# Convolution, SoLU layer and LayerNorm in one kernel: w_in scaled while it is decoded, two chunks convolved in float32, row sums from the product

## The chip, the cores and the metric

The kernel runs on one core of a Trainium2 chip. The metric is the device time of one execution in microseconds. Lower is better. The two weight matrices w_in and w_out are float64 arrays, the other inputs float32. The kernel reads the former as pairs of 32-bit words and decodes exponent, mantissa and sign itself.

## The reference

```python
# x: 8 x 4160 x 192 float32; weight: 8 heads x 7 taps
w = softmax of weight over its 7 taps
out[b, s, h, :] = sum over k of w[h, k] * x_pad[b, s + k, h, :]   # causal, 24 channels a head
x = out.reshape(33280, 192)
h = x @ w_in                                   # 192 x 1024
sm = exp(h - max h) / (sum of exp + 1e-9)
solu = h * sm
ln = (solu - mean) / sqrt(var + 1e-6) * g_ln   # over the 1024 columns
return (ln @ w_out).astype(float32)            # 1024 x 192
```

## The kernel before

The 33280 rows are 260 tiles of 128 rows. They come in 17 chunks: the first batch as 1024, 1056 and 2080 rows, each later batch as two of 2080. For a chunk, x is loaded in windows of 112 rows (plus 16 rows of overlap), five windows to a piece `xr` (`load`, line 125). `sum_squares` gives a scale `s` for the chunk: squares on ScalarE in chunks 0 and 1, maxima on VectorE from chunk 2 on. `halve_steps` splits each piece, times `s`, into a high and a low float16 half (`xs`, lines 211 to 227, nearly all on POOL). `product` (line 260) multiplies them with band matrices `taps_hi` and `taps_lo`, three float16 matmuls for each head, into PSUM. `upper` (ScalarE, line 280) and `lower` (VectorE, line 289) write the result as float16 halves `y`, and `turn` (line 312) transposes them by DMA into `yT`.

A tile then goes through these steps:

- `emit_h` (line 714): ten matmuls of 512 columns on the float16 halves `whi` and `wlo` of w_in give the 1024 logits `ph` in PSUM;
- `emit_max` (line 725, VectorE) scales `ph` and takes its extremum, with an accumulator; `emit_exp` (line 732, ScalarE) writes `e` and its sum;
- `emit_mul` (line 785, VectorE) writes h e over `e`; `emit_hi` (line 790, ScalarE) and `emit_lo` (line 799, POOL) split it into float16 halves `p`, which a DMA transposes into `pT` (line 801);
- `emit_square` (line 794, ScalarE) sums the squares;
- five tiles later `emit_out` (line 813): 24 matmuls with the halves `ohi` and `olo` of the centred w_out. These have 194 columns: 192 of w_out, one of ones, which gives the row's sum, and one of zeros. `emit_evac` (line 821) copies the result out of the one PSUM bank `po`;
- every eight tiles `Group.roots` (lines 867 to 877, POOL) and `row` (lines 882 and 886) scale the rows and store them.

The order is that of the program: `step(i)` issues the work around tile i in a fixed order to the engines' in-order queues, with the tile before it (`cur`) in the steps from the product on. SyncE issues all DMAs, also in order. `chores` spreads the next chunks' work over a chunk's tiles by the fractions in its tables; `chain` and `Queue` hold the scale's steps and the POOL halving.

Before tile 0 the program decodes w_in (`Words`: exponents, mantissas, low words, signs; POOL adds mantissa and low word), sums its squares, takes a power of two `t_in` as its scale and splits it. w_out is decoded beside the first tiles: `out_values` multiplies by the gains, then `out_squares`, `out_mean` (line 674, ones-matmuls in float32) and `out_halves` (lines 689 to 696) centre, scale and split it. In steps 0 to 2 a tile's product stands in its own step (`WARM = 3`), and step 3 has none.

## Time and profile before

| | before |
|---|---|
| median of 3 runs | 1287.07 us (1286.88 to 1289.79) |
| profiled execution, and its span | 1289.18 us, 1287.5 us |
| busy: TensorE, VectorE, ScalarE, POOL | 93%, 78%, 73%, 77% |
| granted TensorE clock, mean | 0.982 |
| DMA queue 1: packets, bytes, share of 16 engines | 724318, 221 MB, 88.3% |

A line of the groups or of the timeline names the source line, engine, operation, out<-in tiles and shapes. In the timeline the first two numbers are the start and the duration in us, and the bracket at the end is how long the engine was idle before, and what ended that. PE is TensorE's matmuls, PEld its weight loads, DVE VectorE, ACT ScalarE, SPq SyncE's queue. A float32 matmul is recorded as two.

### The profile page before, as it was taken

How to read it: one execution, taken by the hardware profiler on the slowest of the kernel's cores; microseconds unless marked ns; L12 is line 12 of the kernel's file. 1: busy time of each engine (PE TensorE's matmuls, PEld its weight loads, DVE VectorE, ACT ScalarE, POOL GpSimd, SP SyncE). 2: the span in 40 equal slices, each digit the busy share in tenths (PEclk: the TensorE clock that was granted, in tenths of full speed). 3: DMA queues.
4: the chain of work that ended last, by engine and by line, in shares of the span. 5: the costliest groups of instructions: out<-in, count | busy, mean ns of one | idle time of the engine just before them, and what ended most of it. 6: DMA issues, size and time to landing. Idle time of an engine off the chain costs nothing. (4 is left out here: it accounts for less than half of the span.)

```text
span 1287.5 us, 25290 instructions
## 1 busy us (share of the span) xinstructions
PE 1195.9 (93%) x9334; PEld 848.4 (66%) x9334; DVE 999.2 (78%) x1881; ACT 937.3 (73%) x1507; POOL 984.9 (77%) x935
## 2 busy tenths in 40 slices
PE   2567899799999999999999999999999999999996
PEld 1344576577777677777776677667676767767675
DVE  8965798578787888878787878788787777776666
ACT  6465677577877777787877777787777778777773
POOL 6543769597897869798896969798796979866665
PEclk9888999899999999999999999999999999999998
DMA  7365798889989898999979899998979898897977
GB/s 212 66 145 117 142 195 159 169 168 187 204 162 210 160 211 176 186 202 171 212 146 203 163 196 198 169 195 158 214 146 201 190 175 157 153 171 144 189 157 145
DMA packets 724442, 222.78 MB, mean 173 GB/s; under 512 B 650894, under 2 KB 724062, under 8 KB 724190
## 3 DMA queue, kind: packets, MB, share of 16 engines
q1 hardware_dynamic: 724318, 221.17, 88.3%
q8 instruction: 73, 1.20, 0.4%
q14 instruction: 51, 0.42, 0.1%
HBM read 33.00 MB, written 25.56 MB: 45 GB/s over the span
## 5 line engine op out<-in xcount | busy, mean ns | idle before, releaser
L799 POOL TENSOR_TENSOR p<-e,p 128x1024 f16<-128x1024 f32 x258 | 551.0, 2138 | 243.9 <-ACT p L790 243.1
L813 PE MATMUL po<-ohi,pT 128*128 128x194 f16 x4160 | 571.3, 248 | 17.7 <-DVE raw L821 7.6
L813 PEld LDWEIGHTS <-pT 128*128 128x128 f16 x6240 | 534.8, 98 | 73.2 <-DMA pT<-p 14.3
L813 PE MATMUL po<-olo,pT 128*128 128x194 f16 x2080 | 512.6, 246 | 0.8 <-DVE olo L696 0.8
L725 DVE TENSOR_SCALAR_CACHE_REDUCE ph<-ph,cv 128x1024 f32<-128x1024 f32 x248 | 320.0, 1291 | 177.3 <-PE ph L714 176.6
L714 PEld LDWEIGHTS <-yT 128*128 128x128 f16 x2600 | 251.4, 98 | 278.5 <-DMA yT<-y 20.7
L732 ACT ACTIVATE e<-ph,sm 128x1024 f32<-128x1024 f32 x259 | 288.0, 1112 | 176.2 <-DVE ph L725 166.0
L714 PE MATMUL ph<-whi,yT 128*128 128x512 f16 x1560 | 385.5, 383 | 19.5 <-DMA yT<-y 16.8
L790 ACT CAST p<-e 128x1024 f16<-128x1024 f32 x259 | 269.3, 1040 | 115.1 <-DVE e L785 68.6
L785 DVE SCALAR_TENSOR_TENSOR e<-ph,cv,e 128x1024 f32<-128x1024 f32 x247 | 315.5, 1277 | 1.4 <-ACT e L732 1.3
L714 PE MATMUL ph<-wlo,yT 128*128 128x512 f16 x1040 | 269.8, 382 | 4.5 <-DVE wlo L612 4.5
L794 ACT ACTIVATE sq<-e 128x1024 f32<-128x1024 f32 x259 | 273.0, 1054 | 0.0
L289 DVE SCALAR_TENSOR_TENSOR y<-pc,y 112x456 f16<-112x456 f32 (+4 forms) x156 | 80.4, 533 | 63.4 <-ACT y L280 55.0
L227 POOL TENSOR_TENSOR xs<-xr,xs 128x960 f16<-128x960 f32 (+1 forms) x63 | 121.8, 1934 | 2.5
L821 DVE COPY raw<-po 128x194 f32<-128x194 f32 x257 | 89.8, 350 | 3.0 <-PE po L813 3.0
L280 ACT ACTIVATE y<-pc 112x456 f16<-112x456 f32 (+2 forms) x140 | 68.2, 499 | 32.5 <-PE pc L260 11.1
L260 PE MATMUL pc<-xs,taps_hi 128*112 128x456 f16 (+1 forms) x256 | 69.5, 353 | 14.3 <-POOL xs L227 6.1
L166 DVE TENSOR_REDUCE xa<-xr 128x1 f32<-128x384 f32 x120 | 73.0, 619 | 0.0
L224 POOL TENSOR_SCALAR xr<-xr,s 128x960 f32<-128x960 f32 (+1 forms) x63 | 65.8, 1045 | 1.9
L886 DVE TENSOR_SCALAR_CACHE_REDUCE o<-raw,t 128x192 f32<-128x192 f32 x133 | 53.1, 404 | 12.7 <-POOL t L877 12.7
L260 PEld LDWEIGHTS <-taps_hi 128*112 128x112 f16 x288 | 37.0, 139 | 38.4 <-issue 8.9
L213 POOL TENSOR_SCALAR xs<-xr,s 128x960 f16<-128x960 f32 (+1 forms) x54 | 55.7, 1032 | 4.4 <-DVE s L101 4.4
(152 smaller groups left out, 633.8 us busy)
## 6 DMA issues: line engine op xcount, KB each, us to landing
out_dram<-o SPq DMA_DIRECT2D x128, 192.0 KB, 2.7
xr<-in_x_dram SPq DMA_DIRECT2D x41, 480.0 KB, 4.6
xr<-in_x_dram SPq DMA_DIRECT2D x22, 384.0 KB, 3.9
pT<-p SPq DMA_TRANSPOSE x259, 4.5
yT<-y SPq DMA_TRANSPOSE x99, 3.8
raw_out<-in_moe_w_out_dram SPq DMA_DIRECT2D x1, 1536.0 KB
raw_in<-in_moe_w_in_dram SPq DMA_DIRECT2D x1, 1024.0 KB, 9.0
xr<-in_x_dram SPq DMA_DIRECT2D x8, 84.0 KB, 3.5
```

Of the source, the lines that this page charges most:

```text
L227: (2.1 * size + 0.2, lambda: pool.tensor_tensor(xl, r, h, ALU.subtract)),
L260: nc.tensor.matmul(o, taps[:, h + j, :], r, start=q == 0, stop=q == len(ops) - 1)
L289: dve.scalar_tensor_tensor(self.at(D, h * HD, e, z, a, b), pc[:, :, e:z], 1.0 / TAPS, self.at(0, h * HD, e, z, a, b), ALU.mult, ALU.subtract,)
L714: nc.tensor.matmul(t.ph[:, n * 512 : (n + 1) * 512], lhs, w[:, r, n * 512 : (n + 1) * 512], start=(j == 0), stop=(j == len(ops) - 1),)
L725: dve.tensor_scalar(t.ph, t.ph, t.cv[:, 0:1], None, ALU.mult, ALU.min, accum_out=t.bias)
L732: act.activation(t.e, t.ph, AF.Exp, bias=t.bias, scale=-1.0, accum_out=grp.z[:, g : g + 1])
L785: dve.scalar_tensor_tensor(t.e, t.ph, t.cv[:, 3:4], t.e, ALU.mult, ALU.mult)
L790: act.copy(t.p16[:, :, 0, :], t.halves)
L794: act.activation(junk, t.e, AF.Square, accum_out=t.grp.s2[:, t.g : t.g + 1])
L799: eng.tensor_tensor(t.p16[:, :, 1, :], t.halves, t.p16[:, :, 0, :], ALU.subtract)
L813: nc.tensor.matmul(t.po[:, 0:WX], t.pT[:, a, :], w[:, c, :], start=(j == 0), stop=(j == len(ops) - 1),)
L821: dve.tensor_copy(t.grp.raw[:, t.g, :], t.po[:, 0:WX])
```

## The change

- w_in: its top rows come in two transfers. `largest` takes the maximum of the raw high words' magnitudes while the words arrive; the power of two `t_in` is worked out from that and added to the exponents' bias (`bias_in`), so the decoded values are already scaled. `join` (VectorE) puts mantissa and low word together in place of POOL's two steps. Two of `whi`'s blocks are copied between partitions by DMA.
- Chunks 0 and 1 (`exact`) are convolved from the unscaled float32 pieces with float32 `taps`: one matmul in place of three, with the chunk's scale applied in `upper` and `lower`. Chunk 2 takes its scale from squares on ScalarE, no longer from maxima on VectorE.
- w_out: its scale comes from the squares of the decoded exponents and the largest gain; the work is spread over steps 0 to 2 in another order. The products of tiles 0 to 2 stand one step later, as all others do, and tile 0's low half is VectorE's.
- The row sum comes from an accumulator in `emit_mul`; `ohi` and `olo` have 192 columns.
- The pool of `xr` has 9 buffers, not 11; `emit_h` takes the blocks in another order; the reciprocal in `root_power` goes.

On POOL (GpSimd), from its last memset on: before, w_in's decoding, chunk 0's and chunk 1's halving stand among the first tiles' low halves `p`.

```order
L485 TENSOR_SCALAR m_in<-m_in 128x1024
L490 TENSOR_TENSOR f_in<-m_in,raw_in 128x1024
L485 TENSOR_SCALAR m_in<-m_in 128x512
L490 TENSOR_TENSOR f_in<-m_in,raw_in 128x512
L224 TENSOR_SCALAR xr_1_87<-xr_1_87,s_164 128x960
L227 TENSOR_TENSOR xs_180<-xr_1_87,xs_180 128x960
L609 TENSOR_SCALAR whi<-f_in,t_in 64x512 x2
L485 TENSOR_SCALAR m_out<-m_out 128x1536
L490 TENSOR_TENSOR f_out<-m_out,raw_out 128x1536
L213 TENSOR_SCALAR xs_329<-xr_0_94,s_298 128x960
L224 TENSOR_SCALAR xr_0_94<-xr_0_94,s_298 128x960
L799 TENSOR_TENSOR p_0_333<-e_330,p_0_333 128x2x512
```

On POOL, the same place in the changed kernel; the last rows are chunk 2's first piece.

```order
L514 TENSOR_TENSOR f_out<-m_out,raw_out 128x1536
L810 TENSOR_TENSOR p_1_399<-e_344,p_1_399 128x2x512
L810 TENSOR_TENSOR p_2_465<-e_407,p_2_465 128x2x512
L810 TENSOR_TENSOR p_3_547<-e_462,p_3_547 128x2x512
L810 TENSOR_TENSOR p_4_614<-e_544,p_4_614 128x2x512
L810 TENSOR_TENSOR p_5_673<-e_611,p_5_673 128x2x512
L217 TENSOR_SCALAR xr_0_282<-xr_0_282,s_592 128x960
L220 TENSOR_TENSOR xs_681<-xr_0_282,xs_681 128x960
```

One operation of w_out is left of the decoding, the halving of chunk 1 is gone, and tile 0's low half has left the engine.

On VectorE, before, from tile 0's product to tile 1's: w_out's values stand ahead of tile 1's maximum.

```order
L785 SCALAR_TENSOR_TENSOR e_330<-ph_304,cv_165,e_330 128x1024
L505 SCALAR_TENSOR_TENSOR e_out<-raw_out,e_out 128x1536
L642 SCALAR_TENSOR_TENSOR f_out<-f_out,gl,e_out 128x192 x8
L725 TENSOR_SCALAR ph_382,sm_393<-ph_382,cv_165 128x1024
L289 SCALAR_TENSOR_TENSOR y_0_203<-pr_349,y_0_203 112x5x64
L289 SCALAR_TENSOR_TENSOR y_0_203<-pr_349,y_0_203 112x5x32
L289 SCALAR_TENSOR_TENSOR y_0_203<-pr_362,y_0_203 112x5x32
L289 SCALAR_TENSOR_TENSOR y_0_203<-pr_362,y_0_203 112x5x64
L785 SCALAR_TENSOR_TENSOR e_402<-ph_382,cv_165,e_402 128x1024
```

On VectorE in the changed kernel, from tile 1's maximum to tile 1's product.

```order
L733 TENSOR_SCALAR ph_331,sm_342<-ph_331,cv_194 128x1024
L793 SCALAR_TENSOR_TENSOR e_326,s_0_300<-ph_304,cv_194,e_326 128x1024
L529 SCALAR_TENSOR_TENSOR e_out<-raw_out,e_out 128x1536
L681 SCALAR_TENSOR_TENSOR f_out<-f_out,gl,e_out 128x192 x8
L810 TENSOR_TENSOR p_0_347<-e_326,p_0_347 128x2x512
L665 TENSOR_REDUCE osq<-gl 128x1
L666 TENSOR_TENSOR osq<-osq 128x1
L667 TENSOR_TENSOR osq<-osq 128x1
```

Tile 1's maximum now stands ahead of tile 0's product and of w_out's values, tile 0's low half behind them; the product has a second output, its row sum.

On ScalarE, before, from tile 2's exp to tile 3's.

```order
L732 ACTIVATE e_434,z_300<-ph_421,sm_432 128x1024
L790 CAST p_2_437<-e_434 128x2x512
L794 ACTIVATE sq_442,s_0_301<-e_434 128x1024
L693 ACTIVATE ohi<-f_out,t_out 128x4x192 x2
L280 ACTIVATE y_1_485<-pc_0_0_486 112x10x48
L732 ACTIVATE e_497,z_300<-ph_474,sm_493 128x1024
```

On ScalarE in the changed kernel, between the same two exps.

```order
L740 ACTIVATE e_407,z_299<-ph_387,sm_405 128x1024
L805 ACTIVATE sq_414,s_0_301<-e_344 128x1024
L172 ACTIVATE xj_1_416,xa_382<-xr_0_94 128x576
L172 ACTIVATE xj_3_418,xa_382<-xr_1_96 128x576
L172 ACTIVATE xj_0_424,xa_423<-xr_0_282 128x384
L172 ACTIVATE xj_1_426,xa_423<-xr_0_282 128x576
L172 ACTIVATE xj_2_428,xa_423<-xr_1_284 128x384
L285 ACTIVATE y_1_441<-pc_0_0_442,s_421 112x5x96
L740 ACTIVATE e_462,z_299<-ph_430,sm_448 128x1024
```

Two sums of chunk 1 and three of chunk 2 (`xj`) stand between the exps now, and the output's high halves have moved ahead of tile 2's exp.

The diff, cut to its core:

```diff
...
 
         bits = dst.bitcast(I32)
-        half = 127 << 22
         return [
             lambda: dve.tensor_scalar(dst, src, tiny, 1.0 / num, ALU.max, ALU.mult),
-            lambda: dve.reciprocal(dst, dst),
             lambda: dve.tensor_scalar(
                 bits, bits, EXPO, 1, ALU.bitwise_and, ALU.logical_shift_right
             ),
-            lambda: dve.tensor_scalar(bits, bits, float(half), None, ALU.add),
+            lambda: dve.tensor_scalar(
+                bits, bits, -1.0, float(380 << 22), ALU.mult, ALU.add
+            ),
             lambda: dve.tensor_scalar(bits, bits, EXPO, None, ALU.bitwise_and),
         ]
...
             q = nc.sync
             a, z = self.cuts[j], self.cuts[j + 1]
             t = xp.tile(
-                [P, PW, D], F32, name=f"xr_{self.ch}_{j}", tag="xr", bufs=11
+                [P, PW, D], F32, name=f"xr_{self.ch}_{j}", tag="xr", bufs=9
             )
             self.raw[j] = t
             first = (self.b * S + self.t0 - HALO) * D
...
             for j in range(n):
                 o = pc[:, :, j * HD : (j + 1) * HD]
                 sl = slice((h + j) * HD, (h + j + 1) * HD)
+                if self.exact:
+                    piece = self.raw[self.cuts.index(a)][:, 0 : z - a, sl]
+                    ops.append((0, j, o, taps, piece))
+                    continue
                 xh, xl = (q[:, a:z, sl] for q in (self.xh, self.xl))
                 ops += [
                     (0, j, o, taps_hi, xh), (2, j, o, taps_hi, xl), (1, j, o, taps_lo, xh)
                 ]
             if bank_given:
                 ops.sort(key=lambda q: q[:2])
-            for q, (_, j, o, taps, r) in enumerate(ops):
+            for q, (_, j, o, tp, r) in enumerate(ops):
                 nc.tensor.matmul(
-                    o, taps[:, h + j, :], r, start=q == 0, stop=q == len(ops) - 1
+                    o, tp[:, h + j, :], r, start=q == 0, stop=q == len(ops) - 1
                 )
             return pc
+        def scale(self):
+            return self.s[0:CW] if self.exact else 1.0 / TAPS
...
     nc.sync.dma_start(wb, weight.partition_broadcast(TJ))
     for j in range(chunks[0].np):
         chunks[0].load(j)
-    nc.sync.dma_start(
-        raw_in[:, 0:F, :].rearrange("p f t -> p (f t)"), w_in[0 : 2 * R, :]
-    )
+    for j in range(NH):
+        nc.sync.dma_start(
+            raw_in[:, j * 512 : (j + 1) * 512, :].rearrange("p f t -> p (f t)"),
+            w_in[0 : 2 * R, j * F : (j + 1) * F],
+        )
...
+    taps = cp.tile([P, H, CW], F32, name="taps")
...
+    def words(c):
+        wi.mantissas(c)
+        wi.exponents(c)
+        wi.join(c)
+    def valued(c):
+        wi.signs(c)
+        wi.value(c, dve)
...
+    for j, c in enumerate(halves):
+        wi.largest(c, floor[:, j : j + 1])
+        words(c)
+        if j == 0:
+            for f in chain0[1:-4]:
+                f()
+    wi.largest(Z, floor[:, 2:3])
+    dve.tensor_reduce(iq[:, 0:1], floor, AX.X, ALU.max)
+    dve.tensor_scalar(
+        iq[:, 0:1].bitcast(I32), iq[:, 0:1].bitcast(I32), 0x7FF00000, None,
+        ALU.bitwise_and,
+    )
+    dve.tensor_scalar(
+        iq[:, 0:1].bitcast(I32), iq[:, 0:1].bitcast(I32), 8.0,
+        -896.0 * 2.0**23, ALU.mult, ALU.add,
+    )
+    dve.tensor_tensor(iq[:, 1:2], iq[:, 0:1], iq[:, 0:1], ALU.mult)
+    tp = total(iq[:, 1:2], "wi")
...
+    dve.tensor_scalar(
+        bias_in, t_in.bitcast(I32), 1.0, -(916.0 + 127.0) * 2.0**23,
+        ALU.mult, ALU.add,
+    )
+    for c in halves:
+        wi.powers(c, bias_in)
+    c0.open(0, None)
+    settle(*spans0[0], got0)
...
+    words(Z)
+    wi.powers(Z, bias_in)
+    for c in halves:
+        valued(c)
+    for pc, hg in got0:
+        c0.upper(pc, *hg)
+    valued(Z)
...
+    for c in halves:
+        act.copy(whi[:, 0, c], wf[:, c])
+        lower_in(wlo[:, 0, c], wf[:, c], whi[:, 0, c])
+    nc.sync.dma_start(whi[top, 2, :], whi[low, 0, :])
+    nc.sync.dma_start(whi[low, 1, :], whi[top, 0, :])
+    act.copy(whi[top, 1, 0:HF], wf[top, Z])
...
+    def out_squares():
+        junk = sp.tile([P, F], F32, name="oj", tag="sq", bufs=1).bitcast(F16)
+        act.activation(
+            junk[:, 0 : NFC * D], wo.e.bitcast(F32), AF.Square, scale=2.0**20,
+            accum_out=osq[:, 0:1],
+        )
+    def out_scale():
+        gm = osq[:, 1:2]
+        dve.tensor_reduce(gm, gl, AX.X, ALU.max, apply_absolute_value=True)
+        dve.tensor_tensor(gm, gm, gm, ALU.mult)
+        dve.tensor_tensor(gm, gm, osq[:, 0:1], ALU.mult)
+        tp = total(gm, "wo", mean)
...
         ops = [
-            (y[0], whi, 0), (y[1], whi, 1), (y[2], whi, 2), (y[0], wlo, 0),
+            (y[0], whi, 0), (y[0], wlo, 0), (y[2], whi, 2), (y[1], whi, 1),
             (y[1], wlo, 1),
         ]
...
     def emit_mul(t):
-        dve.scalar_tensor_tensor(t.e, t.ph, t.cv[:, 3:4], t.e, ALU.mult, ALU.mult)
+        dve.scalar_tensor_tensor(
+            t.e, t.ph, t.cv[:, 3:4], t.e, ALU.mult, ALU.mult,
+            accum_out=t.grp.s1[:, t.g : t.g + 1],
+        )
...
-            s1 = self.raw[:, :n, D]
+            s1 = self.s1[:, :n]
...
         c1, c2, c3 = (chunks[ch + j] if ch + j < NCH else None for j in (1, 2, 3))
         if c1:
-            stage(c1, *((0.4, 0.65, 0.8), (0.19, 0.6, 0.8), (0.25, 0.75, 0.95),
+            stage(c1, *((0.375, 0.7, 0.85), (0.19, 0.6, 0.8), (0.25, 0.75, 0.95),
                         (0.0625, 0.65, 0.9))[min(ch, 3)])
         if c2 and ch < 3:
-            sums(c2, *((0.125, 0.35), (0.0, 0.4), (0.0, 0.25))[ch])
+            sums(c2, *((0.3, 0.55), (0.0, 0.4), (0.0, 0.25))[ch])
         if c3:
             put(0.5 if ch == 0 else 0.0, 0.9 if ch < 2 else 0.7, "load",
                 [(c3, j) for j in range(c3.np)])
...
-    WARM = 3
-    outs = {3: 0, 4: 1, 6: 2, 8: 3}
+    outs = {3: 0, 4: 1, 5: 2, 7: 3}
+    c1_sums = [
+        lambda h=h: chunks[1].sum_squares(*h)
+        for j in range(chunks[1].np) for h in chunks[1].halves(j)
+    ] if NCH > 1 else []
     def step(i):
         t = tiles[i] if i < NT else None
-        cur = i if i < WARM else i - 1 if i > WARM else NT
-        cur = tiles[cur] if cur < NT else None
+        cur = tiles[i - 1] if 0 < i <= NT else None
         k = outs.get(i, None) if i < DEPTH + 4 else i - DEPTH
         done = tiles[k] if k is not None and k < NT else None
         work = {}
...
         if convs:
             first = convs[0][0], conv(*convs[0])
         add_up(i, first[0].bank if first else None)
-        if i == NT - 1:
+        if i in (2, NT - 1):
             emit_mul(cur)
             emit_hi(cur)
+        if i == 2:
+            out_upper()
         if t:
             emit_max(t)
         if i == 0:
+            wo.exponents(W)
+            settle_rest()
+            wo.whole(W)
+        if i < 4:
             run_chain(20)
-        if i == 1:
-            settle_rest()
         if first:
             first[0].upper(first[1][0], *first[1][1])
             first[0].lower(first[1][0], *first[1][1])
         if t:
             (emit_exp if i < NT - 1 else last_exp)(t)
-        if cur and i < NT - 1:
+        if cur and i != 2 and i < NT - 1:
             emit_mul(cur)
             emit_hi(cur)
         if i == 0:
-            queue.run(2.0)
+            wo.powers(W, rebias)
+            out_squares()
+        if i == 1:
             out_values()
         if cur and cur.grp.n == 1 and i < NT:
             emit_z(cur)
...
             if i == NT - 1:
                 emit_evac(done)
         if cur and i < NT:
-            emit_lo(cur, pool if i < NT - 1 else dve)
+            emit_lo(cur, pool if 1 < i < NT - 1 else dve)
         if i == NT - 1:
             emit_z(t)
             last_split(t)
         run_chain(6 if t and t.n < 12 else 4)
-        if i == 0:
-            upper_rest()
+        if i == 1:
+            out_scale()
+        if i == 2:
+            out_lower()
         if done and done.grp.n > 1 and i != NT - 1:
             emit_evac(done)
         run_rows(i)
...
             second[0].lower(second[1][0], *second[1][1])
         if cur and i < NT:
             emit_square(cur)
-        if i == 1:
-            out_squares()
-        if i == 2:
-            out_mean()
-            out_halves()
+        if i in (1, 2):
+            for f in c1_sums[i - 1 :: 2]:
+                f()
+            if i == 2 and c1_sums:
+                follow(chunks[1], i)
         for c, h in work.get("sum", []):
             c.sum_squares(*h)
             if c.sums == 2 * c.np:
-                dve.tensor_tensor(c.part, c.part, c.part, ALU.mult)
+                if c.peaks:
+                    dve.tensor_tensor(c.part, c.part, c.part, ALU.mult)
                 follow(c, i)
         if i == NT:
             last_sums(cur)
```

More of the change, by code (lines that the diff above doesn't have):

```diff
@@ new lines @@
+    for c in halves:
[4 more added lines that the diff above has]
+    act.copy(whi[top, 1, 0:HF], wf[top, Z])
+    act.copy(whi[low, 2, HF:F], wf[low, Z])
+    lower_in(wlo[top, 1, 0:HF], wf[top, Z], whi[top, 1, 0:HF])
+    lower_in(wlo[top, 1, HF:F], wf[low, Z], whi[low, 2, HF:F])
+    act.copy(whi[top, 1, HF:F], wf[low, Z])
+    act.copy(whi[low, 2, 0:HF], wf[top, Z])
@@ L626, with settle_rest @@
-    for f in next_sums[2:]:
-        f()
-    wo.powers(W, rebias)
-    wo.heads(W, 1.0)
-    wo.whole(W)
-    lower_in(wlo[:, 0, :], wa, whi[:, 0, :], every)
-    lower_in(wlo[top, 1, 0:HF], wz[top], whi[top, 1, 0:HF], top)
-    lower_in(wlo[top, 1, HF:F], wz[low], whi[low, 2, HF:F], low)
-    for f in chain0[-4:]:
-        f()
+    wo, W = Words(raw_out, "out"), slice(0, NFC * D)
+    wo.lows(W, 2.0**-32)
+    wo.mantissas(W)
+    wo.floats(W)
+    def settle_rest():
+        settle(*spans0[1], got0)
```

297 lines of the change are left out of this document (114 added, 183 removed).

## The prediction

> **What bounds the kernel now.** I read the page first (busy shares and the 40 slices), then the table by stage, then TensorE's waits.
>
> ```profile
> PE 1195.9 (93%) x9334; PEld 848.4 (66%) x9334; DVE 999.2 (78%) x1881; ACT 937.3 (73%) x1507; POOL 984.9 (77%) x935
> PE   2567899799999999999999999999999999999996
> PEclk9888999899999999999999999999999999999998
> ```
>
> ```profile
> core 0: us, PE busy (x) PEld busy (x) DVE busy (x) ACT busy (x) POOL busy (x), PEclk, DMA share, GB/s
> 0.00:20.00 20.00, 4.99 (x34) 4.01 (x34) 14.39 (x25) 13.12 (x29) 11.82 (x20) 1.00 0.90 253
> 20.00:40.00 20.00, 8.35 (x38) 4.53 (x39) 18.95 (x33) 12.38 (x21) 13.10 (x8) 1.00 0.43 118
> 40.00:60.00 20.00, 12.57 (x47) 8.17 (x46) 18.53 (x29) 9.14 (x16) 12.41 (x8) 0.74 0.34 57
> 60.00:80.00 20.00, 15.11 (x105) 10.79 (x103) 16.35 (x37) 10.49 (x17) 5.34 (x3) 0.91 0.40 93
> 80.00:100.00 20.00, 9.44 (x50) 4.38 (x48) 7.41 (x14) 13.12 (x19) 16.26 (x10) 0.74 0.93 191
> 100.00:160.00 60.00, 50.11 (x352) 33.23 (x350) 40.89 (x77) 36.73 (x58) 33.41 (x29) 0.92 0.62 124
> 160.00:1260.00 1100.00, 1077.79 (x8553) 767.79 (x8551) 865.76 (x1620) 832.99 (x1331) 879.39 (x833) 1.00 0.93 180
> ```
>
> Two regimes. From 160 to 1260 us TensorE works 1077.79 of 1100 us: only its own matmuls set the time there. The first 160 us are a start-up in which it works 100.6 of 160 us while VectorE works 37.5 of the 40 us from 20 to 60. The waits (us in total, times, longest) say for whom:
>
> ```profile
> PE ph L714 <- DMA yT<-y: 16.8, 6, 5.5
> PE pt_wi L84 <- ACT wj L571: 7.8, 1, 7.8
> PE mean L674 <- DVE y L289: 7.4, 1, 7.4
> PE pc L260 <- POOL xs L227: 6.1, 2, 4.1
> PE ph L714 <- DVE wlo L612: 4.5, 3, 2.9
> ```
>
> The second and fifth are the decoding and splitting of w_in, the third w_out's, the first and fourth mostly the supply of chunks 1 and 2. The start's milestones (start, duration, engine, what, idle before) are:
>
> ```profile
> 24.43 0.58 PE L84 MATMUL pt_wi<-isq,ones 128*128 128x3 f32 x2 [7.76 <-ACT wj L571]
> 36.88 0.59 PE L714 MATMUL ph<-wlo,yT 128*128 128x512 f16 x1 [0.20 <-DVE wlo L612]
> 38.88 1.11 ACT L732 ACTIVATE e<-ph,sm 128x1024 f32<-128x1024 f32 x1 [4.79 <-DVE xm L188]
> 52.80 5.46 PE L674 MATMUL mean<-f_out,even 128*128 128x192 f32 x16 [7.40 <-DVE y L289]
> 64.23 0.24 PE L813 MATMUL po<-ohi,pT 128*128 128x194 f16 x1 [2.44 <-ACT ohi L693]
> 98.14 0.61 PE L714 MATMUL ph<-whi,yT 128*128 128x512 f16 x1 [4.61 <-DMA yT<-y]
> 108.37 0.35 PE L260 MATMUL pc<-xs,taps_hi 128*112 128x456 f16 x1 [1.94 <-POOL xs L227]
> ```
>
> That is: w_in's scale is summed at 24.43, tile 0's logits are whole at about 37.5, its exp starts at 38.88, the first output matmul at 64.23, and chunk 2's first convolution is complete at 108.4.
>
> **The columns.** 24 output matmuls a tile go from 194 to 192 columns. Their pitch, from the timeline at full clock:
>
> ```profile
> 599.97 0.24 PE L813 MATMUL po<-olo,pT 128*128 128x194 f16 x1
> 600.05 0.33 PE L813 MATMUL po<-ohi,pT 128*128 128x194 f16 x2
> 600.22 0.24 PE L813 MATMUL po<-olo,pT 128*128 128x194 f16 x1
> ```
>
> Three matmuls in 0.25 us are 83 ns each, 0.43 ns a column; 24 x 2 columns are 21 ns a tile, 5.4 us over 260 tiles. Of the matmuls 8553 of 9334 lie in the stretch that TensorE bounds, so 4.9 us count. Bounds: 0, if the pitch isn't the columns' (a weight load of 128 columns stands before each matmul and could set it), and 5.4.
>
> **The row sum in the product.** `emit_mul` gets an accumulator. No product with one is in the trace; the nearest is the maximum of the same 128x1024, which has one, beside the product without:
>
> ```profile
> 50.74 1.28 DVE L725 TENSOR_SCALAR_CACHE_REDUCE ph<-ph,cv 128x1024 f32<-128x1024 f32 x1
> 51.95 0.13 DVE L725 DVE_READ_ACCUMULATOR ph<-ph,cv 128x1 f32 x1
> 51.95 1.34 DVE L289 SCALAR_TENSOR_TENSOR y<-pr,y 112x320 f16<-112x320 f32 x4
> 53.35 1.28 DVE L785 SCALAR_TENSOR_TENSOR e<-ph,cv,e 128x1024 f32<-128x1024 f32 x1
> 54.55 0.54 DVE L166 TENSOR_REDUCE xa<-xr 128x1 f32<-128x384 f32 x1
> ```
>
> The maximum holds VectorE 1.21 us until the next operation, the product 1.20; the accumulator's read runs beside the next one. So I take 0.01 us a tile, 2.6 us of an engine that idles 234 of the 1100 us: nothing on the path. Behind the product on VectorE wait the output's copy, which frees the one `po` bank, and on ScalarE the f16 cast; at the other end each waits the whole 0.13 us, 34 us of VectorE in all, of which a tenth might reach TensorE: +3.4. Less than zero is excluded, since it only adds work.
>
> A rule speaks against this edit: the Trainium skill, "Vector Engine (DVE) Microarchitecture Reference", section "Points that are easy to get wrong", says that a scalar_tensor_tensor with two non-bf16 SBUF sources runs at half throughput, as no read port is left for the accumulator. Here one source is `ph` in PSUM and one is `e` in SBUF, so by its letter it spares this product; no run yet shows it. If it held all the same, it is the first rival.
>
> **w_in.** The sum of squares of the decoded words goes; a maximum over the raw high words stands in its place, the scale enters through the exponent's bias, and POOL loses all its decoding (the order above). What a VectorE operation costs with POOL still and with POOL at work:
>
> ```profile
> 11.64 0.69 DVE L478 TENSOR_SCALAR m_in<-raw_in 128x1024 int32<-128x1024 int32 x1 [1.06 <-DMA raw_in<-in_moe_w_in_dram]
> ...
> 14.78 2.60 DVE L461 TENSOR_SCALAR e_in<-raw_in 128x512 int32<-128x512 int32 x1
> 17.31 0.41 DVE L478 TENSOR_SCALAR m_in<-raw_in 128x512 int32<-128x512 int32 x1
> 21.49 0.68 DVE L505 SCALAR_TENSOR_TENSOR e_in<-raw_in,e_in 128x512 int32<-128x512 int32 x1
> ```
>
> 2.60 against 0.41 for one form of operation; I take 0.41 for one source and 0.68 for two. Both halves of w_in's top must land, which I put at 11.6, when its decoding starts before (first row). x's scale is out of VectorE at about 12.9, as its ones-matmul now stands behind 24 matmuls of the taps. Then five operations on words and four tiny ones: 12.9 + 3.0 + 0.8 = 16.7 for the sum over partitions, not 24.43. Its five-step chain with the bias ends at 18.3, four y corrections (1.34, quoted above for the second half) at 19.6, the rest of w_in's words (1.5) at 21.1, three signs and three products (4.1) at 25.2, four low parts (2.7) at 27.9. The last six matmuls of 512 columns at half clock (512 x 0.43 ns x 2 = 0.44 each) end at 30.5; the maximum and the exp's start add 1.4: **tile 0's exp at 31.9, 7.0 earlier**. Bounds: 3 earlier, if each two-source operation on 512 takes 1.2 as those beside POOL do; 9, if the first half lands at 9.5. The new copies of `whi` between partitions stand on SP's queue before chunk 2's loads; their halves are ready near 24 and needed at 28, so they cost nothing unless they take over 4 us.
>
> The float32 convolution issues 8 matmuls of 120 columns in place of 24 in f16. The `mean` row prices it: 5.46 us for eight of 192 columns, so 3.4 for eight of 120. In chunks 0 and 1 TensorE waits at those places, and POOL loses chunk 1's halving: 0 on the path.
>
> **w_out.** Its squares go before the decoding, so the scale doesn't wait for the values. In the answer on tile `f_out` (min/median/max ns):
>
> ```profile
> L642 DVE SCALAR_TENSOR_TENSOR f_out<-f_out,gl,e_out x8: 404/407/2149, 43.9 to 50.4; 128x192 f32<-128x192 f32 x8
> L689 DVE TENSOR_TENSOR f_out<-f_out,mean x2: 943/945/947, 62.3 to 63.1; 128x768 f32<-128x768 f32 x2
> L696 DVE SCALAR_TENSOR_TENSOR olo<-f_out,t_out,ohi x2: 1004/1018/1033, 64.2 to 65.2; 128x768 f16<-128x768 f32 x2
> ```
>
> VectorE from tile 0's exp on, in the new order: exponents 1.2, four y corrections 1.3, tile 1's maximum 1.2 (its logits come at 34.9, ten matmuls after tile 0's), so 36.1; product 1.2, signs 2.0, eight values at 0.41 (3.3), tile 0's low part 1.2, the squared gain 0.8: 44.6; t_out 1.8, tile 1's product 1.2, two mean subtractions 1.9, tile 2's maximum 1.2, two low parts 2.0: 52.7. But ScalarE's sums of squares now stand between, five or six of these ahead of what TensorE's add-up and the exp of tile 3 need:
>
> ```profile
> L172 ACT ACTIVATE xj<-xr 128x384 f32<-128x384 f32 (+1 forms) x8 | 4.8, 601 | 1.3 <-DMA xr<-in_x_dram 1.1
> L794 ACT ACTIVATE sq<-e 128x1024 f32<-128x1024 f32 x259 | 273.0, 1054 | 0.0
> ```
>
> With these the first output matmul is at about **55, 9 earlier** than 64.23 (bounds 5 and 12). From there to chunk 2's convolution took 44.1 us. The new steps hold eight such sums more on ScalarE (8 x 0.8 with the accumulator's read, +6.4), and lose the step without a tile of the old warm-up (about -5): 45.5, so 100.5, **8 earlier**. That is what I count; the stages behind are the same code. The nine `xr` buffers, not eleven: a load takes the slot of nine pieces before, whose halving is due a chunk earlier, so none waits; 0. The last tiles keep their chain: 0.
>
> **The sum.** -8.0 - 4.9 + 0 = -12.9 on the profiled execution's 1289.18 us (span 1287.5, 1.7 around it), which is 2.1 above the median of 1287.07 shown; on the median that is 1274. Ends: -14 - 5.4 and -4 - 0 + 3.4, so 1268 to 1286.
>
> **The rivals.** *The product halves* (slower). VectorE's 866 us in the long stretch, 33 of which are reads beside other work, plus 1.2 us for the 238 tiles in it (260 x 8553 / 9334) are 1119: it becomes the bound as soon as the product takes over about 2.3 us. At TensorE's present 98% that is 1142, +42, and -8 from the start: 1321. For: the trace lacks the form. The Trainium skill's rule above is the same case. Against: PSUM as one source, and the maximum's 1.21.
>
> *The lead is given back*: the waits at 98.14 and 108.37 follow DMA (0.93 of its time in 80 to 100 us) rather than the tiles, and only the columns stay: 1282. Against: SP's transposes there wait for POOL, which has less to do.
>
> *More*: with POOL free of chunk 1, TensorE's 10 us of idling in 100 to 160 shrink too and the lead grows to 16: 1266.
>
> *The columns do nothing*: the weight loads set 83 ns. Then 1279.
>
> **How the numbers follow.** Forecast 0.65, halved product 0.10, lead given back 0.11, more 0.09, columns nothing 0.05. A measurement here can tell some 0.3% (3.9 us) from no change, so faster is below 1283.2. The lead given back straddles that, 0.06 and 0.05. Faster: 0.65 + 0.09 + 0.05 + 0.06 = 0.85; same 0.05; slower 0.10. The range 1264 to 1284 leaves out the first rival and the ends of two others.
>
> **What would show it.** Right: pitch of the output matmuls 82.5 to 83, product to next operation 1.20 to 1.25 us, first exp near 32, first output matmul near 55, chunk 2's convolution near 100. Wrong: a product above 2 us, an exp of tile 0 after 36, or a lead at 108 that has gone by 240.

## The result, and the profile after

The changed kernel takes 1281.15 us (median of 4, 1280.23 to 1282.26) where the kernel before takes 1287.11: 0.9949 of it, 95% interval 0.9932 to 0.9967, 6.0 us less. The forecast was 1274.0, range 1264 to 1284. On the chip of a later group of runs the same two kernels took 1281.32 and 1290.71 (0.9926, 0.9909 to 0.9942). The gain is clear of the noise; it is 46% of the 12.9 us that were counted in the first group and 73% in the second. The profiled execution took 1280.23 us, its span is 1278.2.

The page of the changed kernel (engines; TensorE's busy tenths; its granted clock) and the table by stage, in the columns of before:

```profile
PE 1193.7 (93%) x9342; PEld 845.0 (66%) x9342; DVE 984.9 (77%) x2129; ACT 940.7 (74%) x1521; POOL 956.5 (75%) x917
PE   5666899899999999999999999999899999999997
PEclk8878999899999999999999999999999999999998
```

```profile
0.00:20.00 20.00, 10.72 (x59) 9.60 (x60) 13.67 (x40) 10.40 (x26) 5.11 (x14) 1.00 0.94 262
20.00:40.00 20.00, 8.02 (x23) 2.70 (x22) 18.38 (x29) 14.84 (x20) 3.48 (x1) 0.78 0.62 144
...
160.00:1260.00 1100.00, 1074.48 (x8589) 763.22 (x8588) 867.87 (x1859) 834.83 (x1335) 879.26 (x836) 1.00 0.96 180
```

POOL's work of the first 40 us fell from 24.9 to 8.6. In the long stretch TensorE does the same share of work (1074 of 1100, 1078 before), but the DMA engines' share there, the last number but one, rose from 0.93 to 0.96. TensorE's waits name the same places, with one that had been seventh now second. First the row of before, then the first three of after:

```profile
PE po L813 <- DMA pT<-p: 5.7, 6, 1.5
```

```profile
PE ph L722 <- DMA yT<-y: 15.2, 4, 5.2
PE po L824 <- DMA pT<-p: 10.4, 11, 1.8
PE pc L262 <- POOL xs L220: 8.7, 2, 4.5
```

The milestones of the start, from the changed kernel's timeline:

```profile
16.62 0.58 PE L83 MATMUL pt_wi<-iq,ones 128*128 128x1 f32 x2 [0.84 <-DVE iq L589]
31.65 1.11 ACT L740 ACTIVATE e<-ph,sm 128x1024 f32<-128x1024 f32 x1 [1.17 <-DVE ph L733]
55.73 0.32 PE L824 MATMUL po<-ohi,pT 128*128 128x192 f16 x1
98.54 0.35 PE L262 MATMUL pc<-xs,taps_hi 128*112 128x456 f16 x1 [1.72 <-ACT xs L211]
103.43 0.54 PE L262 MATMUL pc<-xs,taps_hi 128*112 128x456 f16 x1 [4.54 <-POOL xs L220]
```

The scale of w_in is summed at 16.62, tile 0's exp starts at 31.65, the first output matmul at 55.73. These three are the prediction's numbers within 0.8 us. Chunk 2's convolution starts at 98.54 and then stands still for 4.54 us. The counterpart of the prediction's milestone of 108.37, for which it forecast 100.5, is the row at 103.43: 4.9 us earlier and not 8. To see what becomes of the lead, the exps of tiles 8, 9, 33 and of the last, first of the kernel before, then of the changed one:

```profile
102.37 1.11 ACT L732 ACTIVATE e<-ph,sm 128x1024 f32<-128x1024 f32 x1 [8.57 <-DVE ph L725]
109.40 1.11 ACT L732 ACTIVATE e<-ph,sm 128x1024 f32<-128x1024 f32 x1
...
239.56 1.11 ACT L732 ACTIVATE e<-ph,sm 128x1024 f32<-128x1024 f32 x1
...
1265.92 0.69 ACT L743 ACTIVATE el<-ph,sm 128x512 f32<-128x512 f32 x1 [0.21 <-DVE ph L725]
```

```profile
94.47 1.11 ACT L740 ACTIVATE e<-ph,sm 128x1024 f32<-128x1024 f32 x1 [7.39 <-DVE ph L733]
104.83 1.11 ACT L740 ACTIVATE e<-ph,sm 128x1024 f32<-128x1024 f32 x1
...
235.49 1.11 ACT L740 ACTIVATE e<-ph,sm 128x1024 f32<-128x1024 f32 x1
...
1259.13 0.69 ACT L751 ACTIVATE el<-ph,sm 128x512 f32<-128x512 f32 x1 [0.22 <-DVE ph L733]
```

The lead is 7.9 us at tile 8, 4.6 one tile later, 4.1 at tile 33, 6.8 at the last tile, and the spans differ by 9.3. So the two profiled executions add up as 4.1 from the start (8.0 counted), 2.7 from the long stretch (4.9 counted) and 2.5 after the last exp (nothing counted). These are single executions: that of before took 2.1 us more than its median and that of after 0.9 less, which is most of the 3.3 us by which 9.3 exceeds the 6.0 of the medians. In the trace of the unedited changed kernel from the later group, the exps of tiles 9 and 33 start at 105.77 and 237.61, 0.9 and 2.1 us later than here, so a term of 2 or 3 us is not exact. Three questions follow: what took half of the start's lead at tile 9, why the columns brought so little, and what happened at the end.

### The profile page after: what moved, and what is told of

It reads as the page before. It is cut to its first block, busy times and chain, and to the rows that moved or that the text cites. A ratio compares the mean times of both kernels' runs of the same rounds, so it can differ in the third digit from the quotient of the medians.

```text
span 1278.2 us, 25553 instructions
## 1 busy us (share of the span) xinstructions
PE 1193.7 (93%) x9342; PEld 845.0 (66%) x9342; DVE 984.9 (77%) x2129; ACT 940.7 (74%) x1521; POOL 956.5 (75%) x917
## 5 line engine op out<-in xcount | busy, mean ns | idle before, releaser
L810 POOL TENSOR_TENSOR p<-e,p 128x1024 f16<-128x1024 f32 x257 | 547.8, 2134 | 255.2 <-ACT p L801 254.5
L824 PE MATMUL po<-ohi,pT 128*128 128x192 f16 x4160 | 564.1, 248 | 18.1 <-DMA pT<-p 10.4
L824 PEld LDWEIGHTS <-pT 128*128 128x128 f16 x6240 | 527.8, 99 | 73.3 <-DMA pT<-p 21.6
L824 PE MATMUL po<-olo,pT 128*128 128x192 f16 x2080 | 515.3, 248 | 0.0
L722 PE MATMUL ph<-whi,yT 128*128 128x512 f16 x1560 | 428.1, 384 | 19.2 <-DMA yT<-y 15.2
L722 PE MATMUL ph<-wlo,yT 128*128 128x512 f16 x1040 | 313.3, 383 | 0.9 <-DVE wlo L621 0.9
L294 DVE SCALAR_TENSOR_TENSOR y<-pc,y 112x456 f16<-112x456 f32 (+2 forms) x150 | 77.6, 534 | 73.0 <-ACT y L285 72.7
L220 POOL TENSOR_TENSOR xs<-xr,xs 128x960 f16<-128x960 f32 (+1 forms) x60 | 115.3, 1921 | 2.4
L832 DVE COPY raw<-po 128x192 f32<-128x192 f32 x257 | 90.2, 351 | 4.2 <-PE po L824 4.2
L285 ACT ACTIVATE y<-pc 112x456 f16<-112x456 f32 (+1 forms) x135 | 65.7, 498 | 31.9 <-PE pc L262 10.7
L262 PE MATMUL pc<-xs,taps_hi 128*112 128x456 f16 x240 | 66.5, 357 | 18.3 <-POOL xs L220 8.7
L217 POOL TENSOR_SCALAR xr<-xr,s 128x960 f32<-128x960 f32 (+1 forms) x60 | 61.5, 1025 | 1.7
L886 POOL TENSOR_TENSOR t<-t,mhalf 128x8 f32<-128x8 f32 (+3 forms) x34 | 54.3, 1597 | 2.7
```

The source lines that it names most:

```text
L220: (2.1 * size + 0.2, lambda: pool.tensor_tensor(xl, r, h, ALU.subtract)),
L262: nc.tensor.matmul(o, tp[:, h + j, :], r, start=q == 0, stop=q == len(ops) - 1)
L294: dve.scalar_tensor_tensor(self.at(D, h * HD, e, z, a, b), pc[:, :, e:z], self.scale(), self.at(0, h * HD, e, z, a, b), ALU.mult, ALU.subt ...
L722: nc.tensor.matmul(t.ph[:, n * 512 : (n + 1) * 512], lhs, w[:, r, n * 512 : (n + 1) * 512], start=(j == 0), stop=(j == len(ops) - 1),)
L810: eng.tensor_tensor(t.p16[:, :, 1, :], t.halves, t.p16[:, :, 0, :], ALU.subtract)
L824: nc.tensor.matmul(t.po[:, 0:D], t.pT[:, a, :], w[:, c, :], start=(j == 0), stop=(j == len(ops) - 1),)
```

## The experiments

Four kernels ran on one chip, four on a second, four on a third, with the kernel before beside each group: 1291.19, 1290.71 and 1291.61 us. Times of one group compare directly; between groups the ratio to the kernel before does.

**The row sum alone.** In the kernel before, the product gets its accumulator; the 194 columns stay.

```diff
-        dve.scalar_tensor_tensor(t.e, t.ph, t.cv[:, 3:4], t.e, ALU.mult, ALU.mult)
+        dve.scalar_tensor_tensor(
+            t.e, t.ph, t.cv[:, 3:4], t.e, ALU.mult, ALU.mult,
+            accum_out=t.grp.s1[:, t.g : t.g + 1],
+        )
```

> The kernel before, with the accumulator in the product alone: 24 output matmuls of 194 columns stay, and the roots read the row sums from the accumulator. Theory (both terms of the forecast are halved, the accumulator costs nothing): the profile after shows 1204 ns from the product to the next VectorE operation where it was 1191 to 1196 before, 10 ns a tile on an engine that idles; the time stays within 1 us of 1287.1. Rival (the accumulator eats what the columns bring): 260 reads of about 0.08 to 0.13 us ahead of the output's copy reach TensorE in part, +2 to +3.4 us.

Unlike what the expectation says, the roots still read the column of ones in this kernel: the accumulator alone was added. Measured: 1290.89, 1.0004 of the kernel before (0.9989 to 1.0019). The accumulator costs nothing that can be measured; a cost above 2.5 us lies outside the interval, one of 2 us does not. (The tile for the sums also moves the transposes' source `p16` from 96 to 64 modulo 256 bytes, here and in the next kernel; what such places do is shown further down.) In the changed kernel's timeline the next operation follows the product after 1.20 us (606.11 to 607.31), as without:

```profile
606.11 1.27 DVE L793 SCALAR_TENSOR_TENSOR e<-ph,cv,e 128x1024 f32<-128x1024 f32 x1
607.31 0.08 DVE L793 DVE_READ_ACCUMULATOR e<-ph,cv,e 128x1 f32 x1
607.31 0.15 DVE L100 TENSOR_SCALAR s<-s 128x1 int32<-128x1 int32 x1
```

**The row sum and the columns.** The same with output matmuls of 192 columns, and the roots reading the accumulator.

```diff
-                t.po[:, 0:WX], t.pT[:, a, :], w[:, c, :],
+                t.po[:, 0:D], t.pT[:, a, :], w[:, c, 0:D],
...
-            s1 = self.raw[:, :n, D]
+            s1 = self.s1[:, :n]
```

> The kernel before, with the accumulator in the product and output matmuls of 192 columns; its start is unchanged. Theory: the pitch falls from 83.9 to 82.5 ns (mean of neighbours between 240 and 1260 us), some 7 us of TensorE's work, but waits for the transposed p take over part, as after shows (10.5 us of them for 5.7 in that stretch): the time falls by 2 to 3.5 us, to 1284. Rival 1 (the columns bring their counted 4.9 and the start is what fails): 1282. Rival 2 (the accumulator eats it): no change.

Measured: 1287.70, 0.9971 (0.9957 to 0.9985), 3.2 below the run with the accumulator alone: within the theory's 2 to 3.5. Here too the waits for pT were 7.5 us where the kernel before has 5.7.

These 3.2 us are not the columns' alone, since the edit also changes what the roots read. The last roots on POOL, first with the column of ones, then with the accumulator:

```profile
1283.20 0.20 POOL L873 TENSOR_TENSOR t<-raw 128x2 f32<-128x2 f32 x1 [3.31 <-DVE raw L824]
```

```profile
1269.49 0.20 POOL L873 TENSOR_TENSOR t<-s 128x2 f32<-128x2 f32 x1
```

The wait is gone, and from the last tile's exp to the end it takes 18.8 us where it took 21.5. The end is 2.7 of the 3.2 us by these two traces. The stretch from tile 33's exp to the last is 4.7 us shorter than in the run with the accumulator alone and 2.4 shorter than in the kernel before, so what the columns are worth here is not settled by these runs.

**The columns put back.** The changed kernel with two columns of zeros behind `ohi` and `olo`, multiplied and used by nobody.

```diff
-    ohi = cp.tile([P, NFC, D], F16, name="ohi")
+    ohi = cp.tile([P, NFC, D + 2], F16, name="ohi")
...
-                t.po[:, 0:D], t.pT[:, a, :], w[:, c, :],
+                t.po[:, 0 : D + 2], t.pT[:, a, :], w[:, c, :],
```

> The changed kernel with two padding columns of zeros put back into its output matmuls (194 instead of 192, copied and used by nobody); the start and the accumulator stay. It measures the start alone. Theory: the start's lead is 8 us at tile 8's exp, 4 from tile 9 on, and those 4 reach the end: 1283 to 1284.5, 2 to 3.5 slower than the changed kernel. Rival (the start's lead is lost altogether later on and all of the gain is columns): 1286 to 1287.

Measured: **1269.74**, 0.983 (0.9816 to 0.9844), more than 11 us faster than the changed kernel, with more columns. Neither theory allowed this. The start is the same (tile 20's exp within 1.2 us of the changed kernel's); the gain comes in the long stretch. The DMA part of its page differs (share of the 16 engines' span; median us from issue to landing), first the changed kernel, then this one:

```profile
q1 hardware_dynamic: 724622, 221.43, 91.0%
pT<-p SPq DMA_TRANSPOSE x259, 4.5
yT<-y SPq DMA_TRANSPOSE x99, 3.8
```

```profile
q1 hardware_dynamic: 724622, 221.43, 82.6%
pT<-p SPq DMA_TRANSPOSE x259, 3.8
yT<-y SPq DMA_TRANSPOSE x99, 3.5
```

The same packets and bytes take 1049 us of each DMA engine (0.826 x 1269.4) where they took 1163 (0.910 x 1278.2). What the edit also did is to move every tile behind these two by 64 bytes in a partition. In the built programs `p16`, the source of the transposes, and `pT`, their target, start at 96 modulo 256 bytes in the kernel before, at 192 in the changed one, and at 0 in this one. That became the new theory.

**POOL's queue emptied.** In the changed kernel, the deferred work is done in full at the end of step 7.

```diff
-        queue.run(0.0 if i < 3 else 3.8 if i < 20 else 2.0 if i < NT - 2 else 100.0)
+        queue.run(0.0 if i < 3 else 20.0 if i == 7 else 3.8 if i < 20 else 2.0 if i < NT - 2 else 100.0)
```

> The changed kernel with POOL's queue of deferred work emptied at the end of step 7: the last two halvings of chunk 2 (about 4.5 us of POOL) then stand ahead of tile 7's low part, for which POOL waits idle from 91.5 to 96.7 us, rather than behind it, and the last high part on ScalarE moves ahead of tile 8's exp. Theory (the second half of the lead is lost in this queue): TensorE's waits of 1.72 us at 98.5 and 4.54 us at 103.4 go, tile 9's exp comes at 99 to 101 rather than 104.8, and the time is 4 to 6 us below the changed kernel, 1275 to 1277. Rival (the wait for y at 148 us, which follows DMA and SP, takes the lead back): tile 9's exp comes earlier, tile 20's does not, and the time stays at 1281.

Measured: 1274.76, 0.987 (0.9857 to 0.9883); the changed kernel has 1281.15 and 1281.32 on other chips. By these times it is 6.4 to 6.6 us faster; by the ratios to the kernel before, 0.987 against 0.9949 and 0.9926, some 7 to 10. The theory's 4 to 6 is met and exceeded. POOL in the changed kernel, from its timeline (the low parts are L810, chunk 2's halving L217 and L220):

```profile
88.44 2.00 POOL L220 TENSOR_TENSOR xs<-xr,xs 128x960 f16<-128x960 f32 x1
90.42 1.07 POOL L217 TENSOR_SCALAR xr<-xr,s 128x960 f32<-128x960 f32 x1
96.69 2.12 POOL L810 TENSOR_TENSOR p<-e,p 128x1024 f16<-128x1024 f32 x1 [5.21 <-ACT p L801]
98.78 2.00 POOL L220 TENSOR_TENSOR xs<-xr,xs 128x960 f16<-128x960 f32 x1
100.75 0.90 POOL L217 TENSOR_SCALAR xr<-xr,s 128x768 f32<-128x768 f32 x1
101.74 1.64 POOL L220 TENSOR_TENSOR xs<-xr,xs 128x768 f16<-128x768 f32 x1
```

and with the queue emptied, with tile 9's exp behind it:

```profile
92.23 2.00 POOL L220 TENSOR_TENSOR xs<-xr,xs 128x960 f16<-128x960 f32 x1
94.21 0.91 POOL L217 TENSOR_SCALAR xr<-xr,s 128x768 f32<-128x768 f32 x1
95.20 1.65 POOL L220 TENSOR_TENSOR xs<-xr,xs 128x768 f16<-128x768 f32 x1
97.66 2.13 POOL L810 TENSOR_TENSOR p<-e,p 128x1024 f16<-128x1024 f32 x1 [0.81 <-ACT p L801]
```

```profile
99.43 1.11 ACT L740 ACTIVATE e<-ph,sm 128x1024 f32<-128x1024 f32 x1 [0.36 <-DVE ph L733]
```

POOL had idled 5.21 us in front of tile 7's low part, whose product stands behind tile 8's maximum, while 4.5 us of halving lay queued behind it and TensorE then waited for just that. Tile 9's exp comes 5.4 us earlier and the last 5.7: nothing later takes it back. Tile 33's exp starts at 231.44, 8.1 us before that of the kernel before, which is the lead that the prediction counted.

**The place of the transposed tiles.** An unused tile of 160 or 64 bytes a partition ahead of `p16` (64 below; 40 in place of 16 makes 160) moves `p16`, `pT` and the small tile `of`, which only the last rows use; the changed kernel unedited, and the kernel before with its tiles at 0, ran beside them.

```diff
     def emit_hi(t):
+        if t.i == 0:
+            sp.tile([P, 16], F32, name="gap", tag="gap", bufs=1)
         t.p16 = sp.tile([P, NH, 2, 512], F16, name=f"p16_{t.i}", tag="p16", bufs=3)
```

> The changed kernel once more, unedited, so that the three runs beside it have it on their own chip. All theories: 0.993 to 0.997 of the kernel before; no wait or packet differs from the profile after.

> The changed kernel with 160 unused bytes a partition ahead of the p16 buffers, so that p16 and pT start at 96 modulo 256 as in the kernel before, rather than at 192, where the change's new layout put them. Theory (the place of the transposed tiles in memory sets how long their DMA packets take; the change moved them to a slightly worse place, and that took part of the columns): the 256 byte packets take 921 us of an engine's time as before rather than 945, and the time falls by 1 to 3 us against the changed kernel beside it. Rival (the waits for pT come from the shorter matmuls alone): no change. Second rival (the place of ohi and olo, or another of the tiles that the 194 columns moved, made that kernel fast): no change.

> The changed kernel, 192 columns, with 64 unused bytes ahead of the p16 buffers: p16 and pT alone start at 0 modulo 256, as they happened to in the run with 194 columns, which took 1269.7. Theory of the place: packets of 256 bytes take about 832 us of an engine's time, pT lands in 3.8 us rather than 4.5, and the time is at or below that run's 1269.7: 1264 to 1270, 11 to 17 below the changed kernel. Rival (the columns themselves, or the place of another tile, made that run fast): the time stays within 3 us of the changed kernel.

> The kernel before with 160 unused bytes ahead of its p16 buffers: p16 and pT start at 0 modulo 256 rather than 96. Nothing else is changed. Theory of the place: its waits for pT (5.7 us) and part of those at chunk starts go too, 8 to 11 us below the kernel before, 1277 to 1280 where that takes 1287; and against this the changed kernel at the same place shows what the change itself is worth: 9 to 13 us, the forecast's 12.9 or close to it. Rival: no change, since the kernel before is bound by TensorE alone.

| kernel | place | us | of the kernel before | 95% interval |
|---|---|---|---|---|
| changed | 192 | 1281.32 | 0.9926 | 0.9909 to 0.9942 |
| changed | 96 | 1282.17 | 0.9935 | 0.9920 to 0.9950 |
| changed | 0 | 1263.81 | 0.9787 | 0.9763 to 0.9811 |
| before | 0 | 1275.93 | 0.9893 | 0.9875 to 0.9910 |

The place decides: at 0 the kernel before is 14.8 us faster, more than the 8 to 11 that were expected, and the changed one 17.5. The unedited kernel repeats the result. My guess that the change had moved the tiles to a worse place, and lost time by that, is refuted: at 96, the place of before, the changed kernel is no faster, though its 256 byte packets took 928 us of an engine's time instead of 944 (sums over the trace's 634,960 such packets; 829 at place 0). At place 0 the change itself is worth **12.1 us**, 1275.93 to 1263.81; the changed kernel's six runs there spread from 1256.41 to 1267.4, and the interval of its ratio is 3 us to either side. The tables from 160 to 1240 us of the changed kernel, of it at 0, and of the kernel before at 0, and the wait for pT of the second:

```profile
160.00:1240.00 1080.00, 1054.48 (x8411) 747.94 (x8410) 851.44 (x1821) 819.55 (x1310) 863.29 (x816) 1.00 0.96 180
```

```profile
160.00:1240.00 1080.00, 1068.61 (x8543) 760.34 (x8541) 861.71 (x1848) 834.10 (x1329) 876.98 (x833) 1.00 0.87 182
```

```profile
160.00:1240.00 1080.00, 1066.75 (x8488) 762.95 (x8487) 858.29 (x1612) 832.98 (x1322) 874.45 (x824) 1.00 0.86 182
```

```profile
PE po L826 <- DMA pT<-p: 1.1, 2, 0.7
```

The DMA share falls to 0.87 and 0.86, 132 more matmuls fit into the same 1080 us, and the wait for pT goes from 10.4 us to 1.1.

**Source or target.** The gap split in the changed kernel: `p16` at 0 with `pT` at 192 (first edit, with the 64 bytes ahead of `p16` of above), and the reverse (second edit alone).

```diff
     def emit_lo(t, eng):
...
+        if t.i == 0:
+            sp.tile([P, 48], F32, name="gap_T", tag="gap_T", bufs=1)
         t.pT = sp.tile([P, 2 * NFC, P], F16, name=f"pT_{t.i}", tag="pT", bufs=4)
```

```diff
+        if t.i == 0:
+            sp.tile([P, 16], F32, name="gap_T", tag="gap_T", bufs=1)
         t.pT = sp.tile([P, 2 * NFC, P], F16, name=f"pT_{t.i}", tag="pT", bufs=4)
```

> The changed kernel with 64 unused bytes ahead of p16 and 192 between p16 and pT: the transposes' source starts at 0 modulo 256, their target stays at 192. Theory 1 (the read side decides: a row of 128 float16 is 256 bytes, and off its place it takes two pieces): packets of 256 bytes as in the run with both at 0, some 830 us of an engine's time, and 1263 to 1266. Theory 2 (the write side decides): as the changed kernel, 944 us and 1281. Theory 3 (both in part): between.

> The changed kernel with 64 unused bytes between p16 and pT: the target of the transposes starts at 0 modulo 256, their source stays at 192. The other half of the run beside it. Theory 1 (read side): 944 us and 1281, the time of the changed kernel. Theory 2 (write side): 830 us and 1263 to 1266.

Measured: 1265.88, 0.9801 (0.9787 to 0.9814), for the source at 0; 1280.47, 0.9917 (0.9902 to 0.9932), for the target at 0. Packets took 832 and 941 us of an engine's time. The read side decides.

**The repairs together.** The place (64 bytes ahead of `p16`) and the emptied queue, both edits as above; then also `y16`, the source of y's transposes, which stands at 160 modulo 256 in the changed kernel, at 0, with the gap ahead of `p16` adjusted to it.

```diff
             if h == 0 and a == 0:
+                if self.ch == 0:
+                    yp.tile([P, 24], F32, name="gap_y", tag="gap_y", bufs=1)
                 self.y16 = yp.tile(
```

> The changed kernel with both repairs: p16 and pT at 0 modulo 256, and POOL's queue emptied at the end of step 7. Theory (two losses in different places, the start and the long stretch): they add, 1257 to 1259 after 1263.8 with the place alone. Rival (the wait for y at a chunk's start takes the 6 us back once the transposes run faster): 1262 to 1264.

> The run beside it with the source of the other transposes, y16, at 0 modulo 256 too (96 unused bytes ahead of it, 224 rather than 64 ahead of p16). Theory (the read side decides): y lands in under 3.3 us rather than 3.5, packets of 256 bytes fall by another 30 to 60 us of an engine's time, and the waits for y at chunk starts (13.3 us in 4) shrink by 1 to 3 us: 1254 to 1257. Rival (TensorE has nothing left to wait for, or the write side decides, whose rows of 224 bytes can't all be in place): the same time as the run beside it.

Measured: 1256.82, 0.9734 (0.9721 to 0.9747), and **1252.38**, 0.9701 (0.9687 to 0.9714). The losses add, as the theory had it, and the third repair brings 4.4 more: y lands in 3.2 us, and the packets take 810 us of an engine's time where they took 833 in the run beside it, a fall of 23 and not the 30 to 60 that were expected. Its 96 bytes also move `e`, `sq` and other tiles behind `y16`, so that all of the 4.4 comes from `y16` is likely, not shown.

```profile
yT<-y SPq DMA_TRANSPOSE x99, 3.2
```

This last kernel beats both, and takes 3.0% less than the kernel before. TensorE's largest waits in it are still those for yT (11.9 us) and for the mean of w_out (8.1).

## Why the prediction was right or wrong

The direction and the range were right. The forecast itself was 7 us too low, and not for the likely reasons that its rivals named. The rival "the lead is given back" has 1282, within 1 us of the 1281.15 measured; that is luck, as it gives up all of the start's lead and keeps all of the columns, where the traces show part of each and a gain at the end. The ends of the prediction's own sum are 1268 to 1286, not the 1264 to 1284 that it gives as its range; the measured time lies in both.

**The row sum** (0): right, by the run with it alone. The first rival, a product at half throughput, is out: 1.20 us. The rule of the Trainium skill ("Vector Engine (DVE) Microarchitecture Reference", section "Points that are easy to get wrong") by its letter spares a product with one source in PSUM, and the trace agrees; two sources in SBUF were not tried.

**w_in and w_out** (exp at 31.9, first output matmul near 55): right at the three milestones, within 0.8 us. The copies of `whi` between partitions landed in 2.2 us and no wait of the trace is put down to them, as the 4 us condition said.

**The step from the first output matmul to chunk 2's convolution** (-8.0 counted, 4.1 left): this failed. It took the distance of 44.1 us over from before and corrected it by ScalarE's sums and a dropped step, on the ground that the stages behind are the same code. They are, but POOL's deferred halving is not at the same place in them. It starts at 82.21 where it started at 85.00:

```profile
85.00 1.08 POOL L224 TENSOR_SCALAR xr<-xr,s 128x960 f32<-128x960 f32 x1
```

```profile
82.21 1.06 POOL L217 TENSOR_SCALAR xr<-xr,s 128x960 f32<-128x960 f32 x1
```

So it gained 2.8 us where the tiles gained 8; the change puts chunk 2's sums at 0.3 to 0.55 of chunk 0's tiles instead of 0.125 to 0.35, which is the likely cause, though no run undid that alone. In the kernel before, one halving stands behind the low part that waits:

```profile
104.59 2.13 POOL L799 TENSOR_TENSOR p<-e,p 128x1024 f16<-128x1024 f32 x1 [5.36 <-ACT p L790]
106.68 1.64 POOL L227 TENSOR_TENSOR xs<-xr,xs 128x768 f16<-128x768 f32 x1
```

In the changed kernel two fell behind it. That this cost the lead is shown by the emptied queue. The rival "the lead is given back" foresaw the size by half but not the mechanism: it is POOL's order, not DMA.

**The columns** (-4.9 counted, 2.7 in the traces): the size of the work was under-estimated, and its worth over-estimated as far as this pair of traces goes. A tile's 24 matmuls, first and last start, before and after:

```profile
623.03 0.25 PE L813 MATMUL po<-ohi,pT 128*128 128x194 f16 x1
...
624.96 0.24 PE L813 MATMUL po<-ohi,pT 128*128 128x194 f16 x1
```

```profile
598.44 0.24 PE L824 MATMUL po<-ohi,pT 128*128 128x192 f16 x1
...
600.33 0.25 PE L824 MATMUL po<-ohi,pT 128*128 128x192 f16 x1
```

That is 1.93 and 1.89 us; over the 254 tiles in which they stand together the medians are 1929 and 1897 ns, so 32 ns a tile and not 21, 8.3 us over 260 tiles. The row quoted in the prediction had 83 ns a matmul, but a quarter of the 194 column matmuls take 86 to 88. In the run with the row sum and the columns, which multiplies 192 columns but leaves `ohi` and `olo` 194 wide, the median is 1907 ns: the count of columns gives 22 ns, as counted, and the other 10 come with the closer packing, for a cause that no run shows. So the pitch does follow the columns, and the rival by which the weight loads set it is out. What failed is the sentence that from 160 to 1260 us only TensorE's own matmuls set the time: with no matmul changed, the kernel before is 14.8 us faster once its transposes are quick. The same table showed the DMA engines at 0.93, and each tile must pass a transpose on them. The waits for pT grew from 5.7 to 10.4 us; 1.8 of that came in the run with the row sum and the columns, and the rest is not traced to one cause. Where the transposes are quick the columns seem to bring more: 1269.74 with 194 and 1263.81 with 192, both with `p16` at 0, ratios 0.983 and 0.9787, 5.5 us. The two intervals almost touch, and other tiles stand in other places in the first.

**The last tiles** (0): missed, 2.5 us. In the kernel before, the row sum of a tile came out of its output matmuls, so POOL's roots had to wait for the copy of the output; now they have it long before. The run with the row sum and the columns, whose start is unchanged, shows it apart: 2.7 us between the last tile's exp and the end. Before (first row) and after:

```profile
1276.29 0.20 POOL L871 TENSOR_TENSOR t<-raw 128x2 f32<-128x2 f32 x1 [3.32 <-DVE raw L821]
```

```profile
1266.22 0.19 POOL L881 TENSOR_TENSOR t<-s 128x2 f32<-128x2 f32 x1
```

The chain that ended last in the changed kernel is TensorE's last 48 output matmuls with one operation on VectorE behind them, where before several steps of the root stood between. I had followed only that the last tile's own row sums are unchanged, not who read the others'.

**The sum** (-12.9). With the transposes quick in both kernels the change is worth 12.1 us, near the forecast, but not by its terms, so the nearness is luck: in that pair's traces the lead is 6.2 us at tile 9's exp, 1.8 at tile 33's, 9.6 at the last and 12.1 in the spans. The start gives 1.8, the long stretch 7.8 (for the columns, 32 ns x 228 tiles are 7.3), the end 2.5. Where the lead between tiles 9 and 33 goes in that pair was not followed up; part of it is the wait for yT at 148 us, 3.2 against 1.8 us.

## What to carry to other kernels

A busy share of 98% on one engine doesn't make it the only bound: a resource at 93% that every tile passes can take back part of a gain on the first, so ask what the next one is before counting the whole. When work is moved earlier, follow each in-order queue that feeds the next stage and see what stands ahead of it; work that has been ready for long behind an instruction that waits is a loss that no engine's busy time shows. And an edit that changes a tile's size moves every tile behind it: where an experiment comes out far from all theories, compare the addresses.

## What the runs showed of the hardware that was not expected

The time of a DMA transpose from SBUF to SBUF depends on where its source starts: a float16 row of 128 elements, 256 bytes, read from a place that is a multiple of 256 takes 20.6 to 21.0 ns in the mean of all 256 byte packets of these kernels, where it takes 23.0 to 23.8 from 64, 96 or 192 modulo 256 (`y16` was off its place in all of these; with it in place too, 20.4). That is 12% of the time of these packets in the changed kernel (944 to 829 us of an engine), 14.8 and 17.5 us of the two kernels. The place of the target alone changed nothing (23.7). The Trainium skill, "DMA: Bandwidth & Descriptors", section "How a descriptor splits into AXI transactions", says that a transaction must start at a multiple of 256 bytes, and that the first one of a descriptor which starts elsewhere begins at the boundary below it. By that account a 256 byte row that starts off a boundary takes two transactions rather than one, which is worked out from the page. The traces agree in that such rows take longer; they don't show the transactions, and that the read side alone matters is what the two runs with source and target apart show. Whether 96 and 192 differ from each other beyond the packets (928 and 944 us) is not shown: the times are the same.
